# An attention and mixture-of-experts kernel: its own planner orders every engine, eight PSUM banks in one pool, PV and row sums in one run, 128-token transposes

## The chip, the cores and the metric

The kernel runs on one core of a Trainium2 chip. The metric is the device time of one execution in microseconds; lower is better. TensorE (PE) multiplies, VectorE (DVE), ScalarE (ACT) and GpSimd (POOL) do the elementwise work, and SyncE (SP) issues the DMAs. Each engine takes its instructions in order.

## What is computed

All tensors are float32: eight batches, eight heads, 576 tokens, head dimension 64. A causal attention with a decay is followed, on its output, by four single-head attentions ("experts") with a gate that keeps two of the four.

```python
scores = q @ k.T / 8 + (cum[i] - cum[j])     # cum = cumsum(log(clip(f))), causal
attn = softmax(scores) @ v                   # 8 batches x 8 heads
x = attn.transpose(0, 2, 1, 3).reshape(B, S, H * D)
logits = x @ w_gate                          # the best 2 of 4 experts, softmax over them
for e in range(4):                           # causal again, no decay
    ye = softmax(x @ wq[e] @ (x @ wk[e]).T / 8) @ (x @ wv[e]) @ wo[e]
    out += gate[e] * ye
```

## The kernel before

The work is cut into 48 units of two heads: for each batch four attention units ("a", head pairs) and two expert units ("m", expert pairs), with the expert units of batch b after the attention units of batch b+1. A unit goes through these steps:

- *prep*. For attention (`prep_attn`, L260 to L294) k and q of two heads are loaded with 96 tokens to a partition row (`TP = 96`, six blocks), and each block is transposed on PE (L278), three blocks into one bank of `ps_x`. ACT copies each half of a bank out, rounded to fp32r (L286), and DVE subtracts that from the bank for the low part (L287). For experts (`prep_moe`) k and q are 12 accumulated matmuls a bank (L413). A DMA copies the rounded part to a second place (L255), another brings the decay rows (L251, L252).
- *max* (`max_pass`): q·k with the queries as rows, in banks of `ps_m` (L439), row maxima by DVE (L445, L456), transposed on PE (L494), copied by ACT (L496), and written by DMA as one more row of q (L501, by `copy_bits` at L255).
- *scores* (`scores`): k·q in high and low parts in banks of `ps_s` (L525, L526), exp by ACT, causal masks and sums of the blocks by POOL into `R` (L583 to L586).
- *attend* (`attend`, L593 to L637): PV with v as the stationary operand, two heads side by side in 64 columns each. It comes in two runs, `oa` (tokens 0 to 255) and `ob` (256 to 575), which take turns in `ps_o`, a pool of one bank.
- For two units together, *sums* (`row_sums`: ones·R, four heads in 32 columns each, L650, then a chain on DVE to the reciprocals) and *apply* (`apply_rows`: PE spreads the reciprocals, L693, DVE multiplies, L694, ACT rounds to `xh`, L711, and DVE subtracts to `xl`, L712).
- For the experts of a batch once, *front* (`moe_front`: v and gate logits, L337; the gate's values are turned by 16 small matmuls a batch in 32 columns each, L384) and *out* (`project_out`, L734).

Before the units stand constants, and the loading of the weights (`load_weights`, L199), which goes through the six buffers `xh`.

PSUM's eight banks are four pools: `ps_m` two, `ps_s` two, `ps_o` one, `ps_x` three. The order of the program comes from a heap of tasks with due times in units (`PLAN`, `HEAD`, `TAIL`, `W`, L25 to L52; L749 to L803); the Tile framework then places the instructions of each engine by a timeline simulation of its own (`schedule_with_timeline_sim=True`, L819), held by marks such as `high_priority`, `keep_in_program_order` and `together`.

Of the kernel before, what the change touches and what calls it, by code (L numbers as in the profile page):

```python
# [33 lines left out]
TAIL = {
    -8: dict(out=(1.864, 2.55)),
    -4: dict(attend=(1.051, 1.456), sums=(1.012, 0.812), apply=(1.4, 1.45)),
    -3: dict(scores=(1.068, 0.768), attend=(1.87, 2.196)),
    -2: dict(scores=(1.967, 1.822), attend=(2.854, 3.648), sums=(2.123, 3.77), apply=(3.329, 3.149), out=(3.6, 4.173)),
    -1: dict(prep=(1.838, 1.796), front=(1.874, 2.374), max=(1.85, 1.868), scores=(2.483, 2.542), attend=(2.6, 3.38)),
    0: dict(prep=(1.85, 2.2), max=(2.304, 2.35), scores=(2.701, 2.942), attend=(3.319, 4.494), sums=(3.665, 3.673), apply=(5, 5.247), out=(5.218, 5.068)),  # L40
}
HEAD = {
    0: dict(prep=(-1.974, -1.322), vals=(1.004, 0.414), max=(-1.03, -0.74), scores=(-0.519, 0.429), attend=(1.55, 1.972)),
    1: dict(prep=(-2, -1.2), vals=(0.133, 0.562), max=(-0.787, -0.624), scores=(-0.279, 0.521), attend=(0.766, 0.671), sums=(1.728, 1.637), apply=(2.3, 2.4)),
    2: dict(prep=(-2.066, -1.404), vals=(-0.831, 0.329), max=(-1.146, -0.817), scores=(-0.4, 0.615), attend=(1.3, 1.237)),
    3: dict(prep=(-2.127, -0.991), vals=(-0.098, 0.002), max=(-0.99, -0.74), scores=(0.292, 1.009), attend=(1.943, 2.05), sums=(1.567, 1.101), apply=(2.099, 2.035)),
    4: dict(prep=(-1.4, -2.439), vals=(-0.344, 1.188), max=(-1, -0.65), scores=(0.134, 0.898), attend=(1.736, 1.293)),
    5: dict(prep=(-2.1, -1.3), vals=(0.573, 0.47), max=(-1.276, -0.937), scores=(0.414, 1.244), attend=(1.5, 2.202), sums=(1.304, 1.2), apply=(2.077, 2.557)),
    6: dict(prep=(-2.824, -1.093), vals=(0.05, 0.418), max=(-0.846, -0.613), scores=(0.55, 0.85), attend=(1.05, 1.699)),
    7: dict(prep=(-2, -1.2), vals=(-0.294, 0.55), max=(-1.11, -1.581), scores=(-0.15, 0.102), attend=(1.507, 2.517), sums=(1.463, 1.772), apply=(2.544, 2.61)),  # L50
    8: dict(front=(-2.4, -0.175)),
}  # L52

@with_exitstack
def tile_decay_attention_moe(ctx: ExitStack, tc, q, k, v, f, w_gate, wq, wk, wv, wo, out):
# [69 lines left out]
    def constants():  # L125
# [8 lines left out]
        for t in v_att + [v_moe]:  # L134
            nc.gpsimd.memset(t[64:128, 4], 0.0)
# [688 lines left out]
```

## Time and profile before

| | us |
|---|---|
| median of 3 runs (769.22 to 769.9) | 769.79 |
| the profiled execution's span | 768.5 |
| PE busy | 726.0 (94%) |
| DVE busy | 586.7 (76%) |
| ACT busy | 471.5 (61%) |
| POOL busy | 406.5 (53%) |

A span runs from the first instruction to the last of one profiled execution. "Busy" counts the time in which at least one instruction of the engine was under way. A PE matmul's record covers its latency as well, and the next one starts long before it ends; so PE's work is read from the starts, not from the durations, and a busy PE can still be late.

### The profile page before, as it was taken

The numbers are of one execution on the slowest core, as the hardware profiler recorded it, in microseconds if no ns is written. First come the engines' busy times: TensorE is split into PE (matmuls) and PEld (weight loads), VectorE is DVE, ScalarE is ACT, GpSimd is POOL, SyncE is SP. The second block draws the span as 40 slices with busy tenths as digits, with TensorE's granted clock in tenths as the row PEclk, the third lists the DMA queues.
The fourth block names the chain that finished last, engine by engine and source line by source line (L and its number), as shares of the span: only waits on it lengthen the run. The fifth ranks groups of instructions, "written<-read, shape, count | busy, mean of one in ns | idle before, by whom it ended". The sixth has DMA issues, their size and how long they took to land.

```text
span 768.5 us, 16867 instructions
## 1 busy us (share of the span) xinstructions
PE 726.0 (94%) x5704; PEld 592.5 (77%) x5704; DVE 586.7 (76%) x1856; ACT 471.5 (61%) x1151; POOL 406.5 (53%) x770
## 2 busy tenths in 40 slices
PE   4699899999999999999999999999999999999997
PEld 3577589768887788777987778877887879879865
DVE  7678977988688877888778886878777987785733
ACT  5477556767566765676556765667656865555543
POOL 8297644564455564456446544555644564473260
PEclk9999999999999999999999999999999999999999
DMA  8974540544226441365224542265413632202203
GB/s 165 192 146 105 124 107 22 115 92 95 49 49 154 109 109 33 69 147 138 67 53 98 142 110 49 50 144 133 108 33 65 150 88 48 55 19 52 67 15 123
DMA packets 142233, 70.84 MB, mean 92 GB/s; under 512 B 124004, under 2 KB 124484, under 8 KB 142148
## 3 DMA queue, kind: packets, MB, share of 16 engines
q1 hardware_dynamic: 142148, 69.77, 40.3%
q8 instruction: 45, 0.74, 0.4%
q14 instruction: 40, 0.33, 0.1%
HBM read 31.43 MB, written 9.74 MB: 54 GB/s over the span
## 4 chain that ended last, share of the span: by engine, by line
PE 76%; DVE 11%; ACT 4%; DMA 4%; issue 3%; POOL 2%; SPq 0%; DVEq 0%; ACTq 0%
PE pp_m L413 11%; PE ob_a L607 8%; PE pv L337 7%; PE po L734 7%; PE m_a L439 7%; PE s_a L525 6%; PE s_a L526 5%; PE ob_m L607 4%; PE tp_a L278 4%; PE s_m L526 3%; PE s_m L525 3%; PE m_m L439 3%; PE sm_a L650 2%; DVE junk_a L445 2%; DVE ka_a L287 2%
## 5 line engine op out<-in xcount | busy, mean ns | idle before, releaser
L287 DVE TENSOR_TENSOR ka_a<-tp_a,kq 64x288 fp32r<-64x288 f32 x256 | 114.6, 453 | 19.2 <-ACT kq L286 12.6
L286 ACT ACTIVATE kq<-tp_a 64x288 fp32r<-64x288 f32 x256 | 101.1, 403 | 39.7 <-DVE ka_a L287 23.5
L445 DVE CUSTOM_DVE_ANT_0 junk_a<-m_a,mask 128x192 bf16<-128x192 f32 (+2 forms) x192 | 93.5, 487 | 40.8 <-PE m_a L439 22.5
L525 PE MATMUL s_a<-ka_a 128*128 128x320 f32 (+4 forms) x384 | 112.7, 316 | 2.8 <-ACT P_a L545 1.6
L439 PE MATMUL m_a<-kq 128*128 128x320 f32 (+4 forms) x384 | 103.9, 333 | 8.7 <-DVE mxs_a L445 3.9
L526 PE MATMUL s_a<-kq 128*128 128x320 f32 (+4 forms) x384 | 102.2, 298 | 0.5 <-DMA kq<-ms_a 0.5
L420 ACT ACTIVATE kq<-pp_m 64x288 fp32r<-64x288 f32 x128 | 51.8, 405 | 70.9 <-PE pp_m L413 34.8
L547 POOL TENSOR_SCALAR_AFFINE_SELECT P_a<-P_a 128x256 f32<-128x256 f32 x64 | 26.1, 409 | 125.3 <-ACT P_a L545 125.2
L511 POOL TENSOR_SCALAR_AFFINE_SELECT P_a<-P_a 128x128 f32<-128x128 f32 x128 | 42.1, 332 | 82.3 <-ACT P_a L560 80.5
L439 PEld LDWEIGHTS m_a<-kq 128*128 128x128 f32 (+1 forms) x384 | 65.1, 190 | 19.1 <-DVE mxs_a L445 8.0
L525 PEld LDWEIGHTS s_a<-ka_a 128*128 128x128 f32 (+1 forms) x384 | 69.8, 184 | 11.7 <-issue 4.3
L421 DVE TENSOR_TENSOR ka_m<-pp_m,kq 64x288 fp32r<-64x288 f32 x128 | 58.1, 454 | 24.7 <-ACT kq L420 22.2
L583 POOL TENSOR_TENSOR R_a<-P_a 128x448 f32<-128x448 f32 x64 | 73.3, 1145 | 4.2
L526 PEld LDWEIGHTS s_a<-kq 128*128 128x128 f32 (+1 forms) x384 | 69.0, 183 | 2.5 <-DMA kq<-ms_a 0.7
L607 PE MATMUL ob_a<-P_a,va 128*64 128x320 f32 (+1 forms) x512 | 69.2, 412 | 1.0 <-POOL pl L577 1.0
L445 DVE CUSTOM_DVE_ANT_0 junk_m<-m_m,mask 128x192 bf16<-128x192 f32 (+2 forms) x96 | 46.6, 486 | 16.1 <-PE m_m L439 14.2
L525 PE MATMUL s_m<-ka_m 128*128 128x192 f32 (+2 forms) x192 | 56.8, 316 | 0.5 <-ACT P_m L560 0.2
L607 PEld LDWEIGHTS ob_a<-P_a,va 128*64 128x64 f32 x512 | 33.9, 136 | 30.2 <-POOL pl L577 2.3
L584 POOL TENSOR_TENSOR R_a<-R_a,P_a 128x320 f32<-128x320 f32 x64 | 55.0, 864 | 1.0
L526 PE MATMUL s_m<-kq 128*128 128x192 f32 (+2 forms) x192 | 50.6, 295 | 1.9 <-DMA kq<-ms_m 1.8
L439 PE MATMUL m_m<-kq 128*128 128x192 f32 (+2 forms) x192 | 48.0, 310 | 0.0
L337 PE MATMUL pv<-vh,xh_a 128*128 128x260 f32 x160 | 47.6, 297 | 0.0
(190 smaller groups left out, 2065.5 us busy)
## 6 DMA issues: line engine op xcount, KB each, us to landing
ka_a<-kq SPq DMA_DIRECT2D x64, 288.0 KB
kn_a<-in_k_dram SPq DMA_DIRECT2D x64, 144.0 KB
qn_a<-in_q_dram SPq DMA_DIRECT2D x64, 144.0 KB
ka_m<-kq SPq DMA_DIRECT2D x32, 288.0 KB
va<-in_v_dram SPq DMA_DIRECT2D x64, 128.0 KB
out_dram<-outb SPq DMA_DIRECT2D x32, 256.0 KB
kq<-ex SPq DMA_DIRECT2D x94, 9.0 KB
va<-in_v_dram SPq DMA_DIRECT2D x32, 32.0 KB
```

The lines of the kernel that those rows point to most:

```text
L286: nc.scalar.activation(hv, src, AF.Copy)
L287: nc.vector.tensor_tensor(lo[:, h, gs], src, hv.bitcast(F32), ALU.subtract)
L337: nc.tensor.matmul(pv[:, :NV], l[c][:, t0 : t0 + 128], r[:, c], start=(n == 0), stop=(n == 3 * KC - 1))
L413: nc.tensor.matmul(pp[:, :HS], w[:, c, es], x[c][:, gs], start=(n == 0), stop=(n == 3 * KC - 1))
L421: nc.vector.tensor_tensor(lo[:, h, gs], src, hv.bitcast(F32), ALU.subtract)
L439: nc.tensor.matmul(dst, qB[0:K, h, i0 : i0 + dst.shape[0]], kB[0:K, h, j0:j1], start=True, stop=True)
L445: nc.vector.tensor_tensor_reduce(jk[:, :n], src, mask[:, MW - n :], 1.0, init, ALU.add, ALU.max, acc)
L525: nc.tensor.matmul(dst, kaf[:, c : c + m], qA[:, h, i0:i1], start=True, stop=False)
L526: nc.tensor.matmul(dst, kqf[0:K, c + h * S : c + h * S + m], qB[0:K, h, i0:i1], start=False, stop=True)
L583: g.tensor_tensor(r[:, h, 128:S], q[:, 320:768], q[:, 768:1216], ALU.add)
L584: g.tensor_tensor(r[:, h, 256:S], r[:, h, 256:S], q[:, 1216:1536], ALU.add)
L607: mm = nc.tensor.matmul(dst[64 * h : 64 * h + 64, c0 : c0 + rhs.shape[-1]], vs[h][0:kp, blk], rhs, start=first, stop=last,)
```

## The change

The heap of tasks and the framework's placing go. Every instruction (or short sequence) becomes an `Op` with an engine, a priority key, a cost, its predecessors and its buffers; `Plan.run` walks through time, at each step takes the engine that can start something first, and among what can start within `EPS` of the earliest takes the smallest key. Costs are formulas (`act`, `dve`, `pool`, `dma`, and PE's in `commit`, with a charge for each change of the tile width), results are held to be `SLACK` later than the model says, and the program is emitted in the order of the modelled starts under `tc.manual_schedule()`. Buffers belong to `Ring`s; the eight PSUM banks are one ring, given to whoever comes.

Beside that:

- PV and the sums become one run of a unit, `c`, `b`, `a`, each pinned behind the last. All of it is in 32 columns: a head's 64 values of v are two matmuls. The sums of one unit (two heads in two halves of the tokens) come first, so the run waits for POOL's sums of that unit. It holds two banks, cut at token 224 (`OA`) in place of 256.
- k and q are loaded as nine blocks of 128 tokens (block 4 half k, half q) by six DMAs in place of four; nine transposes and three banks a unit in place of twelve and four. ACT then makes six copies of 384 columns in place of eight of 288; DVE still makes eight subtractions.
- `xl` and `yl` are subtracted on POOL (`SPLIT`).
- The gate's values are turned by DMAs through DRAM (two out, eight back for each batch) and no longer by PE and two DVE copies.
- The decay rows lie in three layers in DRAM, the third of zeros, written once (33 x 128 pieces of 36 bytes); a unit's q rows then bring their own zero row from the fourth unit on.
- The weights come through the two `outb` buffers, with a key of 3.8 to 7 units (before: due from 1 to 4).

```diff
+    def start(self, op):
...
+        t = max(t, f)
+        if op.cost.get("port"):
+            a, z = self.port["POOL" if op.eng == "DVE" else "DVE"]
+            if a <= t < z:
+                t = z
+        return t
...
+                if m != s["mode"]:
+                    s["se"] += 110 if m != 128 else 150
...
+                t0 = min(got, key=lambda x: x[0])[0] + EPS[e]
+                t, _, op = min((x for x in got if x[0] <= t0), key=lambda x: x[1])
...
-    ps_m = ctx.enter_context(tc.tile_pool(name="ps_m", bufs=2, space=PSUM))
-    ps_s = ctx.enter_context(tc.tile_pool(name="ps_s", bufs=2, space=PSUM))
-    ps_o = ctx.enter_context(tc.tile_pool(name="ps_o", bufs=1, space=PSUM))
-    ps_x = ctx.enter_context(tc.tile_pool(name="ps_x", bufs=3, space=PSUM))
+    r_ps = Ring([psum.tile([128, 512], F32, name=f"ps{i}") for i in range(8)], False)
...
+                for c in range(3):
+                    nc.tensor.transpose(
+                        xb.t[:, c * 128 : (c + 1) * 128], nb.t[:, 3 * g + c].rearrange("p h d -> p (h d)"), ident
+                    )
...
+        def run(dst, lhs, rhs, first, last):
+            for i in range(4):
+                nc.tensor.matmul(dst[32 * i : 32 * i + 32], lhs(i), rhs(i), start=first, stop=last)
...
+        c = add("PE", k0, c32(HS), sums, u["summed"], [rb, ob])
+        b = add("PE", k0, c32(OA, OA - 128), first, [], [pb, ob] + vb, c)
+        a = add("PE", k0, c32(S - OA, S - OA, 320, 192, 64), second, u["made"] + vready + u["summed"], [pb, plb, xb, ob, otb, zb] + vb, b)
...
+    with tc.manual_schedule():
+        plan.run()
+
+
+SPLIT = "POOL"
```

## Rows read from the trace of the kernel before

**Rows 1.** The page, busy time of the whole span: us (share) xinstructions.

```profile
PE 726.0 (94%) x5704; PEld 592.5 (77%) x5704; DVE 586.7 (76%) x1856; ACT 471.5 (61%) x1151; POOL 406.5 (53%) x770
```

**Rows 2.** The page, the chain of work that ended last, by engine.

```profile
PE 76%; DVE 11%; ACT 4%; DMA 4%; issue 3%; POOL 2%; SPq 0%; DVEq 0%; ACTq 0%
```

**Rows 3.** Busy time in two stretches: length, PE, PEld, DVE, ACT, POOL, clock, DMA, GB/s.

```profile
0.00:40.00 40.00, 23.10 (x91) 18.18 (x92) 26.07 (x76) 19.30 (x44) 22.28 (x52) 1.00 0.99 178
40.00:740.00 700.00, 680.46 (x5482) 559.33 (x5482) 551.72 (x1761) 440.64 (x1083) 377.03 (x707) 1.00 0.38 88
```

**Rows 4.** Timeline of PE, full-width matmuls (start us, us, what, xcount).

```profile
404.21 0.30 PE L413 MATMUL pp_m<-xh_a,ql 128*128 128x288 f32 x1
404.34 0.36 PE L439 MATMUL m_m<-kq 128*128 128x448 f32 x1
404.54 0.36 PE L525 MATMUL s_a<-ka_a 128*128 128x448 f32 x1
```

**Rows 5.** Timeline of PE around one PV run (64 columns).

```profile
397.69 0.28 PE L439 MATMUL m_m<-kq 128*128 128x256 f32 x1
397.89 2.16 PE L607 MATMUL ob_a<-P_a,va 128*64 128x320 f32 x16
399.88 0.28 PE L607 MATMUL ob_a<-pl,va 128*64 128x64 f32 x4
400.10 0.36 PE L526 MATMUL s_a<-kq 128*128 128x192 f32 x1
400.29 0.33 PE L525 MATMUL s_a<-ka_a 128*128 128x320 f32 x1
```

**Rows 6.** Timeline of PE around one run of sums (32 columns).

```profile
441.19 0.31 PE L526 MATMUL s_a<-kq 128*128 128x320 f32 x1
441.43 1.18 PE L650 MATMUL sm_m<-R_m,ones_col 128*32 128x288 f32 x16
442.54 0.47 PE L278 MATMUL tp_a<-ident,qn_a 96*128 96x96 f32 x3
442.79 0.36 PE L439 MATMUL m_a<-kq 128*128 128x256 f32 x1
```

**Rows 7.** Timeline of PE around one piece of the gate's matmuls.

```profile
295.84 0.28 PE L526 MATMUL s_a<-kq 128*128 128x256 f32 x1
296.05 0.30 PE L384 MATMUL pg<-gt,ident 128*32 128x5 f32 x12
296.27 0.47 PE L525 MATMUL s_a<-ka_a 128*128 128x448 f32 x1
```

**Rows 8.** Groups of PE by shape: busy us, mean ns, idle before.

```profile
L278 PE MATMUL tp_a<-ident,kn_a 96*128 96x96 f32 x192 | 29.5, 270 | 7.7 <-POOL kq L120 5.5 <-DMA kn_a<-in_k_dram 2.2
L650 PE MATMUL sm_a<-R_a,ones_col 128*32 128x288 f32 x256 | 19.0, 412 | 0.0
L384 PE MATMUL pg<-gt,ident 128*32 128x5 f32 x256 | 6.1, 180 | 0.5 <-DVE gt L378 0.5
```

**Rows 9.** Waits of PE: us in total, times, longest us.

```profile
PE m_a L439 <- DVE mxs_a L445: 3.9, 13, 0.6
...
PE tp_a L278 <- DMA qn_a<-in_q_dram: 1.7, 2, 1.3
```

**Rows 10.** Timeline of SP's queue: an issue of the weights.

```profile
21.43 0.69 SPq L226 DMA_DIRECT2D st_v<-in_moe_wv_dram  x1
```

**Rows 11.** Groups of DVE and POOL: busy us, mean ns, idle before.

```profile
L583 POOL TENSOR_TENSOR R_a<-P_a 128x448 f32<-128x448 f32 x64 | 73.3, 1145 | 4.2
L585 POOL TENSOR_TENSOR R_a<-R_a,P_a 128x192 f32<-128x192 f32 x64 | 37.5, 591 | 2.0
L712 DVE TENSOR_TENSOR xl_a<-ot_a,xh_a 128x576 fp32r<-128x576 f32 x32 | 33.6, 1053 | 0.7 <-ACT xh_a L711 0.5
L712 DVE TENSOR_TENSOR yl_m<-ot_m,yh_m 128x512 fp32r<-128x512 f32 x16 | 12.0, 748 | 3.3 <-ACT yh_m L711 3.2
```

**Rows 12.** The page, DMA queue: packets, MB, share of 16 engines.

```profile
q1 hardware_dynamic: 142148, 69.77, 40.3%
```

More of the change, by code (lines that the diff above doesn't have):

```diff
@@ L7 @@
 from concourse import bass_utils, mybir
-from concourse.masks import make_identity
 from concourse._compat import with_exitstack
@@ L34 @@
[L34 to L41, printed above, removed]
@@ new lines @@
+HEAD = dict(
+    adds=(3.8, 0.97, 0.96, 3.02),
+    apply=(0.81, 0.74, -2.09, 0.37),
+    attend=(-5.16, 0.34, -1.19, 3.37),
+    front=(2.68, -1.69, 1.73, -2.34),
+    gate=(1.63, 1.14, 2.59, -1.06),
+    max=(-1.74, 1.55, 0.02, 0.06),
+    mprep=(-0.65, -0.54, -1.3, 0.14),
+    out=(-1.97, 0.34, -3.91, 3.47),
+    prep=(0.56, -0.54, -0.41, 0.11),
+    rows=(-1.89, -0.09, -1.69, 0.76),
+    scores=(0.75, -2.15, 0.31, 0.03),
+    sums=(0.7, -0.77, -0.02, -2.95),
+    vals=(-1.01, 0.11, -0.84, 0.47),
+    weights=(-0.25, 1.13, -5.09, -1.43),
+)
@@ new lines @@
+TAIL = dict(
+    adds=(-1.62, -0.14, -1.24, 4.77),
+    apply=(-0.2, -0.08, -1.62, -4.38),
+    attend=(0.77, 2.73, -2.58, 1.47),
+    front=(0.4, 1.82, -1.64, 2.12),
+    gate=(-6.07, 2.11, -2.34, -1.96),
+    max=(1.82, -1.05, -2.38, -2.31),
+    mprep=(-0.99, -3.45, -1.64, 0.46),
+    out=(0.42, 0.91, 2.05, -1.59),
+    prep=(-2.88, 0.66, 0.31, 0.4),
+    rows=(0.66, -0.65, 1.33, 0.35),
+    scores=(-0.94, -0.44, 0.3, -0.16),
+    sums=(1.07, 3.16, -4.64, 4.32),
+    vals=(-2.77, -3.52, 4.81, 3.23),
+    weights=(-1.85, -0.02, 1.29, 0.3),
+)
@@ new lines, with __init__, buf, t @@
+EPS = dict(PE=33.0, DVE=5.0, ACT=122.0, POOL=111.0, SP=555.0)
+SLACK = dict(PE=99.0, DMA=168.0, V=102.0)
+class Ring:
+    def __init__(self, tiles, in_turn=True):
+        self.tiles, self.in_turn = tiles, in_turn
+        self.free = [(0.0, i) for i in range(len(tiles))]
+        self.asked = self.given = 0
+    def buf(self):
+        b = Buf(self, self.asked)
+        self.asked += 1
+        return b
+class Buf:
+    def __init__(self, ring, turn):
+        self.ring, self.turn, self.slot, self.left, self.end = ring, turn, None, 0, 0.0
+    @property
+    def t(self):
+        return self.ring.tiles[self.slot]
+    def when(self, ahead=0):
+        r = self.ring
+        if len(r.free) <= ahead or (r.in_turn and self.turn != r.given + ahead):
+            return None
+        return sorted(r.free)[ahead][0]
+    def give(self):
+        if self.slot is None:
+            r = self.ring
+            x = min(r.free)
+            r.free.remove(x)
+            self.slot = x[1]
+            r.given += 1
@@ new lines, in tiles, with one @@
+    def tiles(n, shape, name, dtype=F32):
+        return [const.tile(shape, dtype, name=f"{name}{i}") for i in range(n)]
+    def one(shape, name, dtype=F32):
+        return const.tile(shape, dtype, name=name)
+    ident = one([128, 128], "ident")
+    mask = one([128, MW], "mask", BF16)
+    ones_col = one([128, 32], "ones_col")
+    sel = tiles(2, [128, 128], "sel", F32R)
+    up = one([128, E, E], "up")
+    low = one([128, E, E], "low")
+    zero = one([128, 4 * S // 128], "zero")
+    v_att = tiles(3, [128, 5, 2, D], "va")
```

1645 lines of the change are left out of this document (968 added, 677 removed).

## The prediction

> **What bounds the kernel now.** I first read the busy time and the chain of work: PE is busy 94% of the span, the next engine (DVE) 76% [rows 1], and 76% of the chain that ended last lies on PE [rows 2]. Then the stretches: the first 40 us hold 91 matmul records and 23.1 us of busy PE, with the DMA engines 99% busy; the 700 us after that hold 5482 records and 680.46 us, so PE is visibly idle for 19.5 of them, while DVE is busy for 551.7, ACT for 440.6 and POOL for 377.0 [rows 3]. So in 700 of 768 us the time is what PE has to do. What that is, is read from the starts in the timeline: a full-width matmul of 288 columns holds PE for 0.13 us and one of 448 for 0.20 [rows 4], 0.44 ns a column, although each record lasts about 0.3. By that a 192 takes 0.09, a 256 0.12, a 320 0.15. Where PE is late inside its busy time, it shows as starts that are further apart, above all where it changes between full width and column tiles.
>
> **Part 1: runs in column tiles.** Around a PV run, from the start of the 256 before it to the start of the second matmul behind it, 2.60 us pass [rows 5]. The 256 and the 192 take 0.12 and 0.09. The run's first 16 records take 1.99 us for 1152 columns twice (an fp32 matmul has two records), 0.86 ns a column and pass, and its last 64 columns twice 0.11. What is left, 0.29 us, is what it costs to go to column tiles and back. The same on a run of sums: 1.60 us from the 320 to the matmul behind the three transposes, of which 0.15 is the 320, 0.25 the transposes [rows 6], and 1.03 four passes of 288 columns (the 16 records' 1.18, less the 0.41 of one record [rows 8], is three passes of 0.257); 0.17 is left. On a piece of the gate's matmuls: 0.43 us from the 256 to the next full-width one, less 0.12, is 0.31, the piece included [rows 7].
>
> Before there are 96 PV runs (two a unit), 25 of sums (24, one of them in two pieces) and 21 pieces of the gate's 256 records [rows 8], counted in the timeline: 96 x 0.29 + 25 x 0.17 + 21 x 0.31 = 27.8 + 4.3 + 6.5 = 38.6 us, all on PE's own path. After there are 48, in 32 columns like the sums, and none of the gate's: 0.17 to 0.29 each; I take 0.17, the row of the same width, 8.2 us. PV itself goes from two tiles of 64 columns to four of 32, over the same 1600 tokens' columns a unit. A pass of 288 takes 0.257 us in 32 columns [rows 6], 0.89 ns a column, against 0.86 [rows 5]: at most 0.03 ns x 3200 x 48 = 4.6 us more, at least nothing; I take 2. **Net -28 us**, with ends -20 and -31.
>
> The Trainium skill speaks against this part: TensorE: Matmul & The Clock Gate, "Measured speedup vs the span model", gives four packed tiles 3.07 times the speed of one, not 4. By it the runs' 158 us (below) would grow by 48 and the time would be 764 instead of 716; the row of the sums shows no such loss, and for PV in 32 columns no row exists.
>
> **Part 2: transposes.** Three take 0.25 us, 0.083 each [rows 6]; there are 192 records for k [rows 8] and as many for q (12 a unit in 32 units), and afterwards 9 a unit, 96 fewer. They have 128 tokens in place of 96, a form that no row shows. If the time grows with the tokens (0.11), the saving is nil; if not, 96 x 0.083 = 8.0. I take **-8**, since 96 columns at 0.44 ns would be 0.04, half of what is seen: the columns don't set it. ACT loses 64 copies, DVE's subtractions keep number and columns; neither engine sets the end.
>
> **Part 3: the gate by DMA.** PE's share is in part 1; DVE loses 16 small copies. Added are ten DMAs a batch, 80 in all, and two more loads for each of 32 units: 144 issues on SP, up to 0.69 us each [rows 10], 99 us at most of SP's time, in front of the rows that scores wait for. The back copies move 4 bytes a piece, 23,040 pieces in all. No row shows such a piece; by the mean of the queue, 40.3% of 16 engines over 768.5 us for 142,148 packets [rows 12], 35 ns, they take the 16 engines together 50 us, and their share goes from 0.38 [rows 3] to about 0.45; the low end is nothing. I cost it at nothing: the gate is wanted only for the sums of its expert units, and the DMA engines have half their time left. If that cover is gone, it shows as PE waiting for rows of `kq`.
>
> **Part 4: subtractions on POOL.** DVE loses `xl` and `yl`, 33.6 + 12.0 us [rows 11], and the small ends. POOL takes 2.16 ns a column (1145 less 591 ns over 256 columns [rows 11]), so 1.42 us for 576 and 1.28 for 512: 32 x 1.42 + 16 x 1.28 = 66 us, and some 5 for the ends. POOL goes from 377 [rows 3] to about 445 of some 650 us, 68%; DVE from 552 to about 505, 78%, as now. On PE that is nothing, as long as the expert matmuls that read `xl` are not the next thing due.
>
> **Part 5: PV behind POOL's sums.** The run now waits for all sums of its unit, three adds for each head, the longest of 1.15 us [rows 11], where PV waited for masks alone. Queued behind it on PE is everything, and DVE and ACT wait for that. The plan places the run where it believes the adds done, with some slack; then the cost is nothing. If POOL is late, the price is in the rivals. For the run's 3.3 us PE makes no scores and no row maxima, which DVE and ACT, with a fifth and a third of their time free, take up later.
>
> **Part 6: the order, the banks, the head.** PE's visible waits are short; the maxima's, for a bank that DVE has to empty, are 13 with 3.9 us in all and 0.6 at most [rows 9]. One pool lets a matmul use any free bank, and the plan takes what can start first. The idle 19.5 us of the long stretch [rows 3] can shrink by anything from nothing to all of it, or grow (a rival); I take **-15**, about three quarters, because waits this short need only one other matmul or two in front. In the head PE waits 2.2 us for k [rows 8] and 1.7 for q [rows 9] while the weights are loaded in between [rows 10] and the DMA engines are full [rows 3]. Weights due four units in leave that stretch: **-3** of these 3.9, with ends +3 (the extra zero rows and loads) and -8.
>
> **Sum.** 768.5 - 28 - 8 - 15 - 3 = 714.5 us of span. The median of the runs lies 1.3 above the profiled span, so **716**. The low ends (20, 0, 0, +3) make 753, the high ones (31, 8, 19.5, 8) 703.
>
> **Rivals.**
>
> *A plan that is better still.* PE is also late inside its busy time, which idle time doesn't show. If planning takes all of the 19.5, 8 in the head, and 10 to 15 us of such lateness, it is 692 to 697. For it: the plan's costs stand close to the rows (0.44 ns a column; 110 and 150 ns for a change of width). Against: the old order came from a simulation as well.
>
> *Half lost to new waits.* PE's freed time makes all others relatively busier. If PE waits anew for half of the 54 gained, it is 743. For it: every engine's order is fixed beforehand, and one run of 3.3 us takes the place of two shorter ones [rows 5]; against: DVE is no nearer its limit than now.
>
> *Slower: POOL late in front of the run.* The splits of 1.42 us now stand among the adds in POOL's order. If the run of each unit stands at PE's head for one such split, it is 48 x 1.42 = 68 us more, 784. It decides from 54 / 48 = 1.1 us of wait a unit on. For it: `xl` took DVE 1053 ns, more than its 12% more columns than `yl` (748) explain [rows 11], so neighbours on the memory already disturb it; against: POOL is idle for 46% of the long stretch [rows 3].
>
> *Three of four tiles at once.* The runs' work is 48 x (2 x 0.257 + 3200 columns x 0.87 ns) = 158 us. If a new stationary operand for each matmul keeps one tile of four waiting, it is a third more, 53 us: 769, no change. The 0.257 us of the sums [rows 6], which reload theirs too, speaks against it.
>
> *It doesn't do what it says.* If each run falls in two (a wait inside it), 48 more changes of width cost 8 to 14 us: 724 to 730, near the forecast.
>
> **How the numbers follow.** Chances: the forecast with what lies around it (700 to 728) 0.50; the better plan 0.20; half lost (728 to 765) 0.18; three of four tiles, or no change for another reason, 0.03; slower 0.09. The time is the forecast's, 716. Below 688 I leave 0.05, above 750 0.15 (the two last and the end of the half lost), so the range is 688 to 750. Faster by over 0.2% (about what a measurement of this kernel can tell from no change): 0.50 + 0.20 + 0.18 = 0.88; within it 0.03; slower 0.09.
>
> **What would show it.** Part 1: 48 runs in the timeline, with 0.2 to 0.3 us of loss around each. Part 2: transposes that start 0.083 us apart. Parts 3 and 4: no more waits of PE on rows of `kq` than now, POOL near 475 us in all, DVE near 535. Part 5: hardly a wait ahead of the run's first matmul; 50 us there would prove the slower case. Part 6: about 5 us of idle PE in the long stretch. I am wrong if PE's idle time after the first 40 us grew, whatever it is put down to.

## The result and the profile after

| | before | changed |
|---|---|---|
| median of the runs | 769.85 us (769.22 to 771.09) | 723.03 us (721.15 to 723.92) |
| span of the profiled execution | 768.5 us | 721.5 us |
| ratio | | 0.9387 (0.937 to 0.9404) |

The kernel is 6.1% faster; 716 was forecast, in a range of 688 to 750. One correction to the description of the change: a run begins with PV of the later tokens, goes on with the first 224 and ends with the sums (the timeline below shows it so); it does wait for POOL's sums, as was said.

The page of the changed kernel: busy time of the engines, the chain that ended last by engine, the DMA queue. They answer to [rows 1, 2, 12].

```profile
PE 683.9 (95%) x6696; PEld 568.4 (79%) x6696; DVE 530.2 (73%) x1776; ACT 449.4 (62%) x1087; POOL 463.0 (64%) x834
...
q1 hardware_dynamic: 172088, 70.29, 46.6%
...
PE 82%; DVE 4%; ACT 4%; SPq 3%; DMA 3%; issue 2%; POOL 2%; POOLq 0%; DVEq 0%; ACTq 0%
```

The windows of before, cut at 40, 140 and 690 us (the head alone is in [rows 3]):

```profile
40.00:140.00 100.00, 93.85 (x749) 74.77 (x747) 81.78 (x246) 63.05 (x155) 61.73 (x111) 1.00 0.46 97
140.00:690.00 550.00, 538.22 (x4362) 442.99 (x4358) 440.79 (x1425) 352.01 (x866) 296.43 (x562) 1.00 0.39 89
```

and of the changed kernel:

```profile
core 0: us, PE busy (x) PEld busy (x) DVE busy (x) ACT busy (x) POOL busy (x), PEclk, DMA share, GB/s
0.00:40.00 40.00, 20.24 (x70) 14.90 (x71) 28.35 (x84) 13.57 (x26) 18.33 (x46) 1.00 0.83 125
40.00:140.00 100.00, 91.09 (x845) 74.65 (x844) 67.49 (x227) 63.13 (x152) 70.36 (x121) 0.95 0.62 129
140.00:690.00 550.00, 546.02 (x5531) 460.45 (x5533) 425.87 (x1443) 357.40 (x876) 357.27 (x642) 1.00 0.43 93
```

Behind 140 us PE is idle for 4.0 us in 550 where it was for 11.8; but between 40 and 140 us for 8.9 instead of 6.2, and in the first 40 for 19.8 instead of 16.9. Between 40 and 140 us the granted clock is 0.95, where before held 1.00. The waits of PE show what the first 140 us wait for (us in total, times, longest us):

```profile
PE ps L936 <- DMA kq<-ms: 9.2, 4, 3.8
PE ps L635 <- DMA nat<-in_q_dram: 5.7, 4, 2.1
PE ps L635 <- DMA nat<-in_k_dram: 5.0, 1, 5.0
PE ps L910 <- DVE mxs L906: 3.4, 3, 2.5
PE ps L1158 <- ACT rt L1139: 2.3, 6, 0.7
PE ps L1069 <- DMA va<-in_v_dram: 2.2, 2, 1.9
```

**Where 47 us went.** Busy time can't tell it, since records overlap. So the starts of all PE records of a trace were put into a balance. A full-width matmul is charged 0.44 ns a column and 6 ns (at least 85 ns for 96 and more columns, and 109 for a transpose of 128 tokens), four matmuls in 32-column tiles (or two in 64) together 0.83 ns a column; what a run takes beyond that, up to 0.45 us, is charged to the run; all that is left, visible idle time and lateness inside busy time, is the rest. "First" is the rest in the first 140 us, "later" the rest behind it; "low" is for how many us the windows show a granted clock of 0.5. The trace's first record of the clock stands at 40.6 us before and at 43.3 us in the changed kernel, in the others between 10 and 47 us; ahead of it the column reads 1.00, though the starts there show half the rate (last section). So "low" leaves out a first stretch that differs from kernel to kernel, and its figures are not to be compared as they stand; the 3.5 of before begin 0.8 us ahead of that kernel's end. What is missing to a span, 9 to 10 us in every kernel, lies ahead of PE's first and behind its last start.

| kernel | median us | work us | runs: us (number) | rest first | rest later | low |
|---|---|---|---|---|---|---|
| before | 769.85 | 626.4 | 53.0 (141) | 39.1 | 40.4 | 3.5 |
| changed | 723.03 | 624.7 | 15.7 (42) | 48.6 | 23.4 | 11.1 |
| slack of 112 ns | 734.62 | 624.7 | 15.8 (42) | 60.3 | 24.9 | 39.7 |
| runs unpinned | 772.18 | 624.7 | 40.9 (111) | 54.0 | 40.6 | 37.0 |
| 96 tokens | 737.08 | 626.1 | 15.8 (42) | 47.8 | 36.3 | 15.2 |
| subtractions on DVE, new plan | 744.79 | 624.5 | 15.8 (42) | 59.5 | 34.4 | 24.5 |
| subtractions on DVE, same plan | 735.30 | 624.7 | 15.7 (42) | 49.5 | 35.7 | 27.5 |
| four pools of two | 824.40 | 624.7 | 17.3 (48) | 55.7 | 114.6 | 41.0 |
| long zero pieces, new plan | 731.66 | 624.8 | 15.3 (41) | 57.0 | 23.5 | 31.3 |
| long zero pieces, same plan | 717.79 | 624.7 | 15.7 (42) | 42.8 | 23.2 | 17.0 |
| filler | 721.81 | 635.2 | 15.4 (42) | 37.0 | 23.3 | 25.9 |
| all rows from ACT | 721.69 | 624.7 | 15.7 (42) | 42.1 | 29.6 | 9.6 |
| three units' rows from ACT | 715.69 | 624.7 | 15.7 (42) | 41.8 | 23.3 | 10.6 |
| the same with filler | 714.31 | 630.1 | 15.7 (42) | 35.0 | 23.2 | 11.0 |

From before to changed: work -1.7, runs -37.3, rest later -17.0, rest first +9.5, in all -46.5 of the 47.0 us of span. The whole gain is the runs and the long stretch; the first 140 us got worse. The forecast divides the span at 40 us and not at 140. By the same charges, reckoned anew (the sums come within 0.3 us of the table's), the rest up to 40 us is 25.1 before and 26.8 after, and behind 40 us 54.1 and 45.5: +1.7 and -8.6.

A run of the changed kernel in PE's timeline, with the full-width matmuls behind it; it answers to [rows 5, 6]:

```profile
482.83 2.25 PE L1069 MATMUL ps<-P,va 128*32 128x352 f32 x32
484.90 0.29 PE L1069 MATMUL ps<-pl,va 128*32 128x64 f32 x8
485.02 0.73 PE L1069 MATMUL ps<-P,va 128*32 128x224 f32 x16
485.56 0.67 PE L1069 MATMUL ps<-R,ones_col 128*32 128x288 f32 x8
486.16 0.36 PE L935 MATMUL ps<-ka 128*128 128x192 f32 x1
486.35 0.28 PE L936 MATMUL ps<-kq 128*128 128x192 f32 x1
```

The 64 records start one above the other in fours and hold 3776 columns: 3.15 us at 0.83 ns. From the run's start to the start of the second matmul behind it pass 3.52; less 3.15 and 0.09 for the 192 leaves 0.28. The 320 ahead of the run starts at 482.52, so another 0.17 is lost in front. These 0.45 us, the most that the balance charges to a run, are the upper end; the mean of 53.0 us over 141 runs is 0.38, and of 15.7 over 42 it is 0.37. By kind, before: 0.39 for the 95 PV runs in 64 columns, 0.32 for the 24 of sums in 32, 0.41 for the gate's 21 pieces.

The first 32 records, PV in 32 columns, take 2.07 us for 1216 columns twice: 0.85 ns a column and pass, against 0.86 in 64 columns [rows 5]. Over all such steps of 192 columns and more behind 140 us the median is 0.84 in both kernels. (That the balance finds equal work for both widths proves nothing, since it charges both alike.)

### The profile page after: what moved, and what is told of

It is laid out like the page before. It is cut to its first block, busy times and chain, and to the rows that moved or that the text cites. A ratio compares the mean times of both kernels' runs of the same rounds, so it can differ in the third digit from the quotient of the medians.

```text
span 721.5 us, 19147 instructions
## 1 busy us (share of the span) xinstructions
PE 683.9 (95%) x6696; PEld 568.4 (79%) x6696; DVE 530.2 (73%) x1776; ACT 449.4 (62%) x1087; POOL 463.0 (64%) x834
## 4 chain that ended last, share of the span: by engine, by line
PE 82%; DVE 4%; ACT 4%; SPq 3%; DMA 3%; issue 2%; POOL 2%; POOLq 0%; DVEq 0%; ACTq 0%
PE ps L1069 20%; PE ps L804 14%; PE ps L824 10%; PE ps L935 10%; PE ps L936 10%; PE ps L1218 6%; PE ps L702 6%; PE ps L635 4%; PE ps L1158 2%; DMA kq<-ms 2%; SPq L620 1%; ACT kq L584 1%; DVE ka L594 1%; PE ps L910 1%; DVE junk L830 1%
## 5 line engine op out<-in xcount | busy, mean ns | idle before, releaser
L594 DVE TENSOR_TENSOR ka<-ps,kq 64x384 fp32r<-64x384 f32 (+2 forms) x384 | 170.5, 454 | 68.3 <-ACT kq L584 62.2
L584 ACT ACTIVATE kq<-ps 64x384 fp32r<-64x384 f32 (+1 forms) x320 | 140.1, 451 | 45.6 <-PE ps L804 31.1
L936 PE MATMUL ps<-kq 128*128 128x192 f32 (+4 forms) x576 | 157.5, 302 | 9.2 <-DMA kq<-ms 9.2
L935 PE MATMUL ps<-ka 128*128 128x192 f32 (+4 forms) x576 | 164.2, 312 | 1.5 <-ACT P L965 1.1
L830 DVE CUSTOM_DVE_ANT_0 junk<-ps,mask 128x192 bf16<-128x192 f32 (+2 forms) x288 | 132.1, 482 | 30.0 <-PE ps L824 24.9
L936 PEld LDWEIGHTS ps<-kq 128*128 128x128 f32 (+1 forms) x576 | 107.0, 187 | 11.8 <-DMA kq<-ms 10.1
L935 PEld LDWEIGHTS ps<-ka 128*128 128x128 f32 (+1 forms) x576 | 107.6, 187 | 10.3 <-DVE mxs L830 4.0
L1034 POOL TENSOR_TENSOR R<-P 128x448 f32<-128x448 f32 x96 | 110.0, 1148 | 4.1
L824 PE MATMUL ps<-kq 128*128 128x192 f32 (+4 forms) x576 | 107.7, 314 | 2.1 <-DMA kq<-ex 1.2
L824 PEld LDWEIGHTS ps<-kq 128*128 128x128 f32 (+1 forms) x576 | 87.6, 188 | 17.8 <-ACT ot L1110 2.9
L1069 PE MATMUL ps<-P,va 128*32 128x352 f32 (+4 forms) x1632 | 99.5, 381 | 2.2 <-DMA va<-in_v_dram 2.2
L1038 POOL TENSOR_TENSOR R<-R,P 128x320 f32<-128x320 f32 x96 | 82.7, 870 | 0.1
L1116 DVE STREAM_TRANSPOSE zt<-ps 128x288 f32<-128x288 f32 x48 | 23.1, 482 | 39.4 <-ACT ot L1111 39.1
```

What stands on the lines that cost most here:

```text
L584: nc.scalar.activation(dst, bank.t[hs, cols[0][0] : cols[0][0] + z - a], AF.Copy)
L594: nc.vector.tensor_tensor(kab.t[64 * (1 - w) : 64 * (1 - w) + 64, w, h, a - w * S : z - w * S], bank.t[hs, o : o + z - a], kqb.t[0:64, h]. ...
L824: nc.tensor.matmul(dst, kqb.t[:, h, 1, i0 : i0 + dst.shape[0]], kqb.t[:, h, 0, j0:j1], start=True, stop=True)
L830: nc.vector.tensor_tensor_reduce(junk[turn[0] % 2][:, :n], src, mask[:, MW - n :], 1.0, init, ALU.add, ALU.max, acc)
L935: nc.tensor.matmul(dst, kaf[:, c : c + m], kab.t[:, 1, h, i0:i1], start=True, stop=False)
L936: nc.tensor.matmul(dst, kqf[:, c + h * S : c + h * S + m], kqb.t[:, h, 1, i0:i1], start=False, stop=True)
```

## The experiments

**Is it the number of runs?** The three parts of a run as three steps:

```diff
-        c = add("PE", k0, c32(HS), sums, u["summed"], [rb, ob])
-        b = add("PE", k0, c32(OA, OA - 128), first, [], [pb, ob] + vb, c)
-        a = add("PE", k0, c32(S - OA, S - OA, 320, 192, 64), second, u["made"] + vready + u["summed"], [pb, plb, xb, ob, otb, zb] + vb, b)
+        a = add("PE", k0, c32(S - OA, S - OA, 320, 192, 64), second, u["made"] + vready + u["summed"], [pb, plb, xb, ob, otb, zb] + vb)
+        b = add("PE", k0, c32(OA, OA - 128), first, [a], [pb, ob] + vb)
+        c = add("PE", k0, c32(HS), sums, u["summed"] + [b], [rb, ob])
```

> The three parts of a column-tile run (PV of the later tokens, PV of the first 224, sums) are given to the plan as three separate steps that follow each other, instead of one step that nothing may come between. If the saving of Part 1 is that there are fewer changes of tile width (141 runs in the trace of before, 42 in that of the changed kernel, 0.39 us lost around each in both), the time is 723 us + 0.39 us for each run that the trace counts beyond 42: with 90 to 141 runs, 742 to 762 us. Rival: a change costs what the prediction took, 0.17 to 0.29 us, then 731 to 750 us for the same counts. Second rival: the plan puts full-width work between the parts only where PE would have waited, then the time is within 2 us of 723 whatever the count.

Measured: 772.18 us, ratio 1.0037 (1.0016 to 1.0057), all of the gain gone. PE's timeline of this kernel shows a run in pieces, a 256 between them (the sums follow at 414.68, in a third piece):

```profile
409.79 2.25 PE L1069 MATMUL ps<-P,va 128*32 128x352 f32 x32
411.86 0.29 PE L1069 MATMUL ps<-pl,va 128*32 128x64 f32 x8
412.08 0.39 PE L824 MATMUL ps<-kq 128*128 128x256 f32 x1
412.40 0.75 PE L1069 MATMUL ps<-P,va 128*32 128x224 f32 x16
```

The trace counts 111 runs, 69 more, and they take 25.2 us more: 0.37 each, as the theory has it and above the 0.17 to 0.29 of the prediction. That makes 748, though, and 772 was measured: another 22.6 are rest, 5.4 first and 17.2 later. More than the runs got worse, and that asked for the next kernel.

**What is a new plan worth?** No work is changed here, only a number that the plan reckons with:

```diff
-SLACK = dict(PE=99.0, DMA=168.0, V=102.0)
+SLACK = dict(PE=99.0, DMA=168.0, V=112.0)
```

> Nothing of the work changes: the plan alone believes that a result of DVE, ACT and POOL is 112 ns later instead of 102, and orders everything anew from the same table of fitted positions. If the order found by the plan is sensitive to such details (theory: in the three experiments with a new plan, part of the loss of 8 to 22 us is that the fitted table no longer fits), the time is 728 to 740 us, with more waits of PE and more low clock in the first 140 us. Rival: the order is robust, and the losses of those experiments belong to their edits; then 723 within 3.

Measured: 734.62 us, 0.9542 (0.9505 to 0.9578), 11.6 us more for nothing. Nearly all of it is in the first 140 us (rest 11.7 more there, 1.5 behind). There the windows of this kernel show 8.1 us more idle PE, and the granted clock at 0.84 where the changed kernel had 0.95:

```profile
0.00:40.00 40.00, 19.77 (x69) 14.65 (x70) 28.95 (x84) 13.57 (x26) 18.41 (x46) 0.94 0.82 124
40.00:140.00 100.00, 83.44 (x753) 64.14 (x752) 64.20 (x188) 53.35 (x132) 65.89 (x112) 0.84 0.55 121
```

So the table of positions fits one graph of costs; whatever changes a cost deals a new hand in the first 140 us. For the unpinned runs this covers the 5.4 first but not the 17.2 later; what makes those stays open. An experiment that plans anew is read in the column "rest later", or is made again with the order kept. All runs below that are called "same plan" give the plan the costs of the changed kernel and alter only what is issued; PE's order is the same, instruction for instruction, fillers aside.

**Part 2, transposes of 96 tokens again** (four loads, twelve transposes, four banks a unit; a new plan):

```diff
-    BW = 2 * S // 3
+    BW = S // 2
...
-        for g in range(3):
+        for g in range(4):
+            nb = kb if g < 2 else qb
...
-            op = add("PE", key("prep", g / 3), dict(mm=[(128, 128)] * 3), tp, [loads[x] for x in need[g]] + [ready["ident"]], [nb, xb, u["kqb"], u["kab"]])
+            op = add("PE", key("prep", g / 4), dict(mm=[(96, 128)] * 3), tp, [loads[x] for x in need[g]] + [ready["ident"]], [nb, xb, u["kqb"], u["kab"]])
```

> Transposes of 96 tokens again, 12 a unit in place of 9 (384 in all in place of 288), from four loads a unit; all else as in the changed kernel. By Part 2 each of the 96 more costs PE 0.083 us: 8.0 us more, 731 us, with starts 0.083 us apart at either width. Rival: the time of a transpose grows with its tokens, then 12 of 96 cost what 9 of 128 cost and the time stays within 1.5 us of 723. Second rival: the loads by six issues a unit in place of four are what delays the rows of maxima in the first 140 us; then some of the 8 us come back and it is 723 to 728.

Measured: 737.08 us, 0.9567 (0.9538 to 0.9596). The transposes themselves, first in this kernel's timeline of PE, then in the changed kernel's:

```profile
50.24 1.90 PE L636 MATMUL ps<-ident,nat 96*128 96x96 f32 x21
```

```profile
44.03 1.15 PE L635 MATMUL ps<-ident,nat 128*128 128x128 f32 x9
```

One record lasts 0.246 us at 96 tokens and 0.273 at 128, so the last of 21 starts at 51.89 and the last of nine at 44.91: one each 0.083 us, and one each 0.110. Twelve of the one take what nine of the other do, 1.00 and 0.99 us. The rival holds for PE's own time. The 14 us are rest, nearly all of it later (12.9). Whether the fourth bank, the 64 more copies of ACT or the plan make them was not separated; the transposes do not. By the neutral run a new plan alone puts 1.5 behind 140 us, so what this part is worth off PE's own time stays open, and it need not be nothing.

**Part 4, the subtractions on DVE.** With a new plan, and with the same plan:

```diff
-SPLIT = "POOL"
+SPLIT = "DVE"
```

> The subtractions that make the low halves are planned on DVE again, as before the change; all else as in the changed kernel. By Part 4 this is worth nothing on PE: 723 us within 2, with POOL some 66 us less busy (near 400) and DVE some 46 us more (near 576). Rival: DVE is the engine next to the bound, and its lower load is what made PE's waits for maxima and masks go from 13.4 to 4.0 us of idle time behind 140 us; then the time is 728 to 735 with that idle time back. Rival on the other side: POOL is late for the low halves in the first 140 us, then 718 to 721.

```diff
-                    lambda h=h, l=l, xf=xf, cs=cs: (nc.gpsimd if SPLIT == "POOL" else nc.vector).tensor_tensor(l(), xf.t[:, cs], h().bitcast(F32), ALU.subtract),
+                    lambda h=h, l=l, xf=xf, cs=cs: nc.vector.tensor_tensor(l(), xf.t[:, cs], h().bitcast(F32), ALU.subtract),
```

> The subtractions are carried out on DVE, but every instruction stands where the plan for POOL puts it: PE's, ACT's and SP's orders are those of the changed kernel. This is Part 4 alone. Expected by the prediction (worth nothing on PE): 723 to 726 us, with DVE near 578 busy and POOL near 406. Rival: 735 to 745, as with the new plan; then DVE's load is what costs, at some 0.3 us for each of the 64 subtractions.

Measured: 744.79 (0.9673, 0.9645 to 0.9701) and 735.30 (0.9551, 0.952 to 0.9581). At the same order it is 12 us, and the rest later shows the same 12.3. The window of 140 to 690 us of the second kernel, and ACT's group of the preparation's copies in it, to be held against the changed kernel's row that follows:

```profile
140.00:690.00 550.00, 539.90 (x5383) 452.17 (x5381) 455.25 (x1465) 350.49 (x858) 308.85 (x578) 1.00 0.43 92
...
L584 ACT ACTIVATE kq<-ps 64x384 fp32r<-64x384 f32 (+1 forms) x320 | 140.3, 451 | 52.3 <-PE ps L804 28.7 <-DVE ka L594 13.0 <-PE ps L635 7.2
```

```profile
L584 ACT ACTIVATE kq<-ps 64x384 fp32r<-64x384 f32 (+1 forms) x320 | 140.1, 451 | 45.6 <-PE ps L804 31.1 <-PE ps L635 8.4 <-DVE ka L594 3.6
```

DVE goes from 77% to 83% of this stretch, ACT's copies wait 13.0 us for DVE in place of 3.6, and PE makes 148 matmuls fewer in the same 550 us. Its visible idle time grows by only 6 of the 12 us; the other half is lateness that the waits don't list. DVE has 17% of its time free and still costs PE 12 us. The clock is not the cause: behind 140 us the second kernel's trace records 3.4 us at 0.5 (from 620.7 us on), which at half the rate cost 1.7 us at most. Two ends stay open: the order kept is one made for subtractions on POOL (planned for DVE, the rest later is 11.0 above the changed kernel's, with the loss of a new plan in it), and that the delay reaches PE through ACT's copies is read from their waits and was not tested.

**Part 6, the pool of banks** (a new plan):

```diff
-    r_ps = Ring([psum.tile([128, 512], F32, name=f"ps{i}") for i in range(8)], False)
+    r_ps, r_pm, r_s, r_o = (
+        Ring([psum.tile([128, 512], F32, name=f"ps{n}{i}") for i in range(2)], False) for n in "xmso")
```

> The eight banks are four fixed pairs again (transposes and projections; row maxima and gate; scores; PV), each used in turn, and the plan orders everything anew. A new plan alone has cost 8 to 14 us on three occasions (a neutral change of 10 ns of slack: 734.6). Theory of Part 6, one pool is worth its gain because PE's matmul can take any free bank: 735 + some 10 us and more, 745 to 765, with PE's idle time after 140 us back above 13 us and the waits for DVE's and ACT's emptying of banks at the head of the list. Rival: the order alone carries it; then 730 to 740, what a new plan costs.

Measured: 824.40 us, 1.071 (1.0662 to 1.0757): slower than before, and far above either expectation. Window and waits of PE:

```profile
140.00:690.00 550.00, 517.65 (x4868) 407.67 (x4871) 381.37 (x1275) 330.61 (x778) 322.96 (x581) 0.98 0.40 87
...
PE pss L938 <- DMA kq<-ms: 13.5, 9, 5.6
PE psx L637 <- DVE ka L596: 8.6, 9, 1.8
PE psm L826 <- DVE mxt L863: 6.9, 13, 0.9
PE psm L826 <- DVE mxs L832: 5.9, 12, 1.3
```

PE is idle for 32 us of the stretch in place of 4. At the head of its waits in the whole span stand the rows of maxima (13.5 us, where the changed kernel has 9.2), and not the emptying of banks as expected; the three for DVE to empty a bank of a pair come next, with 21.4 together. All but 7 of the 98 us of rest are later, where the new plan of the neutral run cost 1.5. Which split of eight banks would do better was not tried. The pairs here are not those of the kernel before, and the table was fitted for one pool, so the 101 us price this undoing and not the step from before.

**The head: 4224 pieces of 36 bytes.** SP's queue in the changed kernel:

```profile
24.72 0.40 SPq L491 DMA_DIRECT2D ex<-zero  x1
25.17 3.52 SPq L664 DMA_DIRECT2D va<-in_v_dram  x1
28.78 2.45 SPq L376 DMA_DIRECT2D kq<-ms  x2
...
25.00:30.00 5.00, 4.15 (x18) 3.65 (x16) 2.65 (x12) 1.83 (x4) 0.00 (x0) 1.00 1.31 37
```

Behind the zero rows the issue of a load takes 3.52 us, and in that stretch a DMA share of 1.31 moves 37 GB/s (the view counts a packet's whole time where it starts, so a share can pass 1). The row of maxima is issued behind it, and PE waits for that until 36.09. The Trainium skill's page DMA: Bandwidth & Descriptors, "Why small descriptors are slow (HBM only)", puts a fixed cost on each small piece; the row agrees in kind. Long pieces, from a buffer of `R` that DVE clears at its head; made with a new plan and with the same (the diff is that of the second):

```diff
-    ex[2].rearrange("x h s -> x (h s)").rearrange("x (p c) -> p x c", p=128),
-    zero[:, : 2 * S // 128].unsqueeze(1).to_broadcast([128, NP + 1, 2 * S // 128]),
+    ex[2].rearrange("x h s -> x (h s)"),
+    r_r.tiles[2][: NP + 1].rearrange("p h s -> p (h s)"),
```

> One of the three layers of zero rows is written in 33 pieces of 4608 bytes in place of 4224 pieces of 36 bytes; it is the one whose issue stands at 24.7 us, four issues ahead of the row of maxima that PE's scores wait for until 36.1 us (a wait of 4.3 us). If the small pieces hold the DMA engines (37 GB/s at a full share in 25 to 30 us), the row lands 3 to 4.5 us earlier and the time is 718.5 to 720. Rival: the row stands behind the loads of weights and v in any case, or PE is next held by them: 723 within 1.

> The long zero pieces again (33 of 4608 bytes for 4224 of 36), but planned at the old cost, so that every engine's order is that of the changed kernel; one more clearing of a buffer stands at the head of DVE. If the small pieces delay the row of maxima that PE waits for until 36.1 us, that wait of 4.4 us shrinks and the time is 718.5 to 721. Rival (v and q loads hold the row anyway): 723 within 1.5. If it is near 731 as with the new plan, long pieces themselves are worse.

Measured: 731.66 us with the new plan (0.9492, 0.9456 to 0.9528), 717.79 with the same (0.9326, 0.9299 to 0.9352). The first would have condemned the edit; the 13.9 us between the two come with the plan, in which the clearing of the buffer also stands at another place. In the second SP's queue and the same window read

```profile
24.75 0.30 SPq L491 DMA_DIRECT2D ex<-R  x1
25.09 0.41 SPq L664 DMA_DIRECT2D va<-in_v_dram  x1
25.61 1.66 SPq L376 DMA_DIRECT2D kq<-ms  x2
...
25.00:30.00 5.00, 4.32 (x18) 3.82 (x18) 2.81 (x12) 1.83 (x4) 0.00 (x0) 1.00 0.53 125
```

and the second score matmul starts at 31.80 in place of 36.09. All of these 4.3 us reach the end, and 0.9 more: rest first falls by 5.8.

**The clock.** In the changed kernel PE's own timeline shows what happens around one of the other waits for rows of maxima, and the windows the clock (the third number from the end, 0.56 and 0.75):

```profile
68.73 0.36 PE L935 MATMUL ps<-ka 128*128 128x192 f32 x1
71.48 0.53 PE L936 MATMUL ps<-kq 128*128 128x192 f32 x1 [2.39 <-DMA kq<-ms]
71.80 0.52 PE L935 MATMUL ps<-ka 128*128 128x320 f32 x1
72.12 0.47 PE L936 MATMUL ps<-kq 128*128 128x320 f32 x1
...
70.00:75.00 5.00, 3.52 (x14) 3.44 (x15) 4.94 (x20) 2.38 (x4) 4.24 (x10) 0.56 0.40 77
75.00:80.00 5.00, 5.00 (x46) 3.77 (x48) 1.27 (x4) 4.34 (x14) 3.82 (x8) 0.75 0.63 141
```

Behind 2.4 us of idle PE the granted clock is 0.5, the lower level of 1.2 GHz, until 77.5 us: 320 columns take 0.27 us where they take 0.15 at the full 2.4 GHz. Filler in such waits, with the same plan:

```diff
+def filler(dst, *at): [nc.tensor.transpose(dst, ident, ident) for _ in range(FILL.get(at, 0))]
...
+FILL = {("t", 0, 1, 1): 7, ("t", 2, 1, 1): 10, ("t", 2, 1, 2): 6, ("m", 0): 12,
+        ("s", 0, 0): 18, ("s", 1, 0): 20, ("s", 2, 0): 22}
```

> 95 transposes of the identity, whose results are written over, stand in front of seven of PE's waits in the first 100 us (7, 12, 10 and 6 in the first 25 us; 18, 20 and 22 ahead of the scores that wait for rows of maxima at 31.7, 68.7 and 94.2 us), at the same order of all else; each lot is shorter than the wait it fills. Theory: PE's lower rate until 43 us and the granted clock of 0.5 in 70.6 to 77.5 and 97.9 to 101.4 us follow from those waits; with PE at work in them the clock does not fall and the rise comes earlier, 4 to 8 us less in all: 715 to 719. Rival: the clock falls for another reason, or what PE makes earlier waits for the next row: 723 within 2. On the other side: a lot outlasts its wait, up to 4 us more.

Measured: 721.81 us, 0.9376 (0.935 to 0.9401), 1.2 below the changed kernel, inside what these runs can tell from no change. PE does reach the full rate sooner (transposes 0.109 us apart from 11.6 us on), but loses it three times before 45 us (at 13.6, 27.3 and 37.5 us), and again at 71.6; the windows of this kernel show the first:

```profile
10.00:15.00 5.00, 2.26 (x12) 1.44 (x12) 4.67 (x12) 4.31 (x10) 4.61 (x10) 0.86 0.35 80
15.00:20.00 5.00, 4.66 (x20) 3.82 (x19) 4.96 (x22) 0.00 (x0) 4.39 (x12) 0.50 0.96 197
20.00:25.00 5.00, 3.29 (x24) 2.61 (x24) 2.57 (x7) 0.27 (x1) 0.09 (x1) 0.96 0.75 152
```

The theory's 4 to 8 us did not come. The fillers did not hold the clock either, so what a full clock through the head is worth stays open; that PE, when faster, mostly waits longer for transfers would fit and is not shown.

**Rows of maxima from ACT's queue,** on top of the long pieces, with the same plan:

```diff
-            copy_bits(row[:, h, S - 64 : 2 * S].rearrange("o (b c) -> o b c", b=5), mb.t[2][5 * h : 5 * h + 5])
+            nc.scalar.dma_start(row[:, h, S - 64 : 2 * S].rearrange("o (b c) -> o b c", b=5).bitcast(F32), mb.t[2][5 * h : 5 * h + 5].bitcast(F32))
```

> The changed kernel's order, with the long zero pieces (717.8 us by themselves) and with the rows of maxima issued from ACT's queue, right behind ACT's copy that makes them, in place of SP's, where loads of weights, q and k are issued back to back. Theory: the waits for the rows (4.6 us in three places with the long pieces, at 66 and 91 us the largest, with the clock at 0.5 for 10 us behind them) are SP's issues in front: 713 to 716. Rival: the rows land no sooner because the transfers in front hold the DMA engines: 717 to 719. On the other side: issuing holds ACT, whose exponentials come later: up to 4 us more, 722.

Measured: 721.69 us, 0.9362 (0.9329 to 0.9395), 3.9 more than the long pieces alone, with intervals that overlap. The waits for rows did shrink (4.6 to 2.3 us), and the third unit's scores came 5.3 us sooner (85.92 for 91.24), but PE waits for ACT in place of SP:

```profile
PE ps L1158 <- ACT rt L1139: 9.2, 13, 3.5
...
PE ps L936 <- DMA kq<-ms: 2.3, 2, 1.3
```

ACT's issues last 0.7 us each (the median of 96), and the rest later is 6.4 above that of the long pieces. These waits are those of the side "holds ACT" of the expectation. For the first three units alone (and everything else from SP), and once more with 49 fillers:

```diff
-            nc.scalar.dma_start(row[:, h, S - 64 : 2 * S].rearrange("o (b c) -> o b c", b=5).bitcast(F32), mb.t[2][5 * h : 5 * h + 5].bitcast(F32))
+            (nc.scalar if u["n"] < 3 else nc.sync).dma_start(row[:, h, S - 64 : 2 * S].rearrange("o (b c) -> o b c", b=5).bitcast(F32), mb.t[2][5 * h : 5 * h + 5].bitcast(F32))
```

> Long zero pieces at the changed kernel's order, and the rows of maxima from ACT's queue for the first three units alone. With all units (721.7 us) scores came up to 5 us sooner at 86 us, but each issue holds ACT for some 0.7 us and PE then waited 13 times for ACT's rt (9.2 us, among them 0.9 in each of five batches). If that is where the gain went, three units keep the former without the latter: 714 to 716. Rival: the wait of 3.8 us for rt at 93 us stays and takes the gain at once: 717 to 719, the time of the long pieces alone.

> The same and 49 transposes of the identity in front of six of PE's waits in the first 90 us (6, 12, 8 and 5 before 25 us, 8 and 10 ahead of the second and third unit's scores). In the changed kernel 95 of them brought the full clock from 43 to some 9 us and gave 1.2 us; with fewer waits left the clock should fall less often: 1 to 3 us below the run without them, 712 to 714. Rival: the clock falls at other waits as before: within 1 us of it.

(The full rate "from 43 to some 9 us" in the last text is wrong: it came from 11.6 us on, and not for good.) Measured: 715.69 us, 0.929 (0.9273 to 0.9307), and 714.31, 0.9269 (0.925 to 0.9287). Three units are 6.0 us below all units, clear of noise, and 2.1 us below the long pieces alone, with intervals that just overlap: the price is gone, and that a gain is left is likely and not sure. The intervals of the filler's last 1.4 us overlap too. The last kernel is the fastest of the study, 8.7 us below the changed kernel; all of that is rest in the first 140 us (48.6 to 35.0, of which 5.4 went into filler).

## Why the prediction was right, step by step

The time is in the range and 7 us above the forecast; the terms were less right than their sum. That the sum came so near is in part luck: nearly 10 us too little in Part 1 made up for 7.5 too much in Part 2 and 11 too much in Part 6.

| part | forecast | measured | from |
|---|---|---|---|
| 1, runs | -28 (-20 to -31) | -37.7 | balance: runs -37.3, column tiles' work -0.4 |
| 2, transposes | -8 (0) | -0.5 | 384 at 0.083 against 288 at 0.109 |
| 6, long stretch, from 40 us on | -15 | -8.6 | balance, cut at 40 us |
| 6, head, up to 40 us | -3 (-8 to +3) | +1.7 | balance, cut at 40 us |
| sum | -54 | -46.5 | the balance; other work is -0.8, and its two reckonings differ by 0.6 |

**Part 1.** The mechanism is right, the term was mis-sized. The loss around one PV run and one run of sums was read at single places [rows 5, 6], 0.29 and 0.17, with the 0.17 taken for the new run because it has the same width. The mean (0.45 at most counted) is 0.38 before and 0.37 after, and in 32 columns alone it goes from 0.32 (sums) to 0.41 (gate), on both sides of the 0.39 in 64: width does not set it. Both places that were read lie below the mean of their kind. (By its own terms the end of -31 is -30.4.) The number of runs was 42, not 48, since six hold two units. PV in 32 columns cost nothing (0.85 ns a column and pass against 0.86 in 64; 2 us were forecast). So the rival of three tiles in four falls: its third more, 53 us, would show in these steps. The Trainium skill (TensorE: Matmul & The Clock Gate, "Measured speedup vs the span model") gives the 3.07 times for four row tiles; of column tiles, which the runs here are, it lists three, at 2.38 times. The 48 us that the prediction worked out from it did not come; the factor itself isn't measured here, since no run has one tile alone.

**Part 2.** The wrong end was taken. "The columns don't set it" was concluded from 96 columns taking more than their columns' time; but a time above the columns' need not stay the same when tokens are added. It is 0.083 at 96 and 0.110 at 128. The nil end was named and priced (0.11) and was exact for PE's own time. "Neither engine sets the end" of ACT's copies is not shown: with the part undone the rest later grew by 12.9 us.

**Part 3** is right as to the gate: its first DMA is issued at 129.2 us, and PE's long waits for rows of maxima all end by 97.2. But the sign named for a failure, more waits for rows of `kq`, did appear: 9.2 us, where before it was

```profile
PE s_m L526 <- DMA kq<-ms_m: 1.8, 3, 0.8
...
PE s_a L526 <- DMA kq<-ms_a: 0.5, 1, 0.5
```

It came from something that was put under the head at +3 at most: the zero rows in 36-byte pieces, alone worth 5.2 us, and from loads issued back to back on SP.

**Part 4** failed. "On PE that is nothing" holds busy shares against each other: DVE 78%, POOL 68%. At the same order the subtractions on DVE cost 12 us. The busy times came out as forecast (DVE 530 for 535, POOL 463 for 475), so the loads were right and the conclusion from them wrong: an engine at 83% that has to empty banks for PE is late often enough to cost 1.7%, though PE's waits list half of it at most.

**Part 5** is right as far as the waits show: the largest ahead of a run is for v (2.2 us in all); none listed is for POOL's sums. It was not undone. The slower rival, POOL late in front of the run, did not occur.

**Part 6.** Of the 15 us forecast for all behind 40 us, 8.6 came: 17.0 behind 140 us, by lateness as much as by idle time (7.8 of it visible), less about 8 lost between 40 and 140. It is not the order alone: 12.3 hang on Part 4, and with pairs of banks the gain turns into 91 us of loss. How much of the 17.0 the new order makes, and how much one pool in place of the four of before, stays open. The idle 5 us forecast for 40 us onward were 12.9 up to 690, 8.9 of them before 140; before it was 17.9, so the sign "I am wrong if" did not appear. In the head the opposite of the forecast happened; the step that failed is "weights due four units in leave that stretch: -3". They leave the first 40 us, and PE's idle time there grows from 16.9 to 19.8 all the same, with waits for k and q and, to 36.09, for the first row of maxima behind the zero rows. Five weight loads stand on SP's queue at 61 to 88 instead (3.2 us of issues), among loads of k, q and v, where the second and third unit's rows of maxima are due. Which of these loads holds the rows was not tested.

**The rivals.** "Half lost to new waits" (743) is, in number, what the kernel becomes without Part 4 and a fitted order (744.8): new waits of that size are possible, and these two hold them off. That the parts' gains depend on one another in this way was in no term of the sum.

## What to carry to other kernels

Price a change of tile width from the mean over all its places, not from one: here 0.3 to 0.4 us there and back, in 32 columns as in 64, and merging runs was most of the gain. Cut a measurement where the forecast was cut. When a planner's positions are fitted, try an edit at the kept order as well; planned anew, a good one looked 9 us worse and a neutral one 12. Off PE's path, ask how often an engine is late and not how busy it is, and look in each issue queue at what stands in front of the smallest urgent transfer.

## What the runs showed of the hardware that was not expected

- The clock column is not the whole story of PE's rate. In the changed kernel the windows give 1.00 for the first 40 us, yet transposes start 0.213 us apart there and 0.109 from 44 us on: half the rate, as at the lower level. The trace has no record of the clock ahead of 43.3 us, and where there is none the column reads 1.00. The Trainium skill (TensorE: Matmul & The Clock Gate, "Part 1: The HAM clock gate") has an idle PE start at the lower of its two levels, which agrees with the starts and not with that column.
- After the rise, idle PE of 2.4 and of 2.7 us was followed by some 3 to 7 us at 0.5; in the kernel before no such stretch is recorded between 40.6 us and 767.7, 0.8 us ahead of its end.
- One DMA of 4224 pieces of 36 bytes made the next issue on its queue take 3.52 us instead of 0.41.
- The mean of `xl` on DVE, 1053 ns before [rows 11] and 821 in the kernel with the same plan, is no typical time. Shortest, median and longest before:

```profile
L712 DVE TENSOR_TENSOR xl_a<-ot_a,xh_a x32: 742/750/3539, 74.4 to 692.4; 128x576 fp32r<-128x576 f32 x32
```

  Twelve of the 32 began while a two-operand instruction of POOL was under way and took 864 to 3539 ns; the other 20 took 742 to 757. Six of the twelve took 1.43 us, as the one at 405.29, in an add of POOL that had begun at 404.96 and lasted 1.15 us. So the "neighbours" of the prediction's slower rival are, as far as these rows go, POOL's two-operand instructions under way when it begins, and the median is close to what the columns explain (691 for `yl`).
